# Which halves of K and V a decode kernel keeps, with new orders for all engines and wider moving operands at the end

## The chip, the core and the metric

The kernel runs on one core of a Trainium2 chip. The metric is device time in microseconds from one launch; the time before is the median of three runs. The profile is of one further execution.

## What is computed

Four tokens (one new position in each of four sequences) pass twice through the same attention block A and the same gated FFN block B, with a layer norm ahead of each. Attention reads a window of the last 2048 cached positions, for 8 KV heads of width 256, two query heads to each.

```python
def _A_ref(x, k_cache, v_cache, wq, wo):
    W = min(4096, max(256, Sk // 4))                 # 2048 of 8192
    q = (x @ wq).reshape(B, Sq, Hq, Dh).transpose(0, 2, 1, 3)
    k = jnp.repeat(k_cache[:, :, Sk - W:, :], rep, axis=1)
    v = jnp.repeat(v_cache[:, :, Sk - W:, :], rep, axis=1)
    p = softmax(einsum("bhqd,bhkd->bhqk", q, k) * Dh ** -0.5)
    return einsum("bhqk,bhkd->bhqd", p, v).transpose(0, 2, 1, 3).reshape(B, Sq, Hq * Dh) @ wo
def _B_ref(x, w_gate, w_up, w_down):
    return (silu(x @ w_gate) * (x @ w_up)) @ w_down
x = x + _A_ref(_layernorm(x), ...); x = x + _B_ref(_layernorm(x), ...)
x = x + _A_ref(_layernorm(x), ...); x = x + _B_ref(_layernorm(x), ...)
```

Both layers use the same K and V, since there is one cache. A window of K of one token and head is 1 MB in bf16, one of V too: 64 MB for 32 pairs (token, head), and 128 MB if everything is read once in each layer.

## The kernel before

**Pairs and groups.** The unit of work is a triple of digits: token, layer, head ("013" is token 0, layer 1, head 3). `PLAN` lists the 64 triples in 44 stages; "+" or "&" joins two triples of a stage into one group that is computed together, and "&" issues their score matmuls as two operations. There are 50 groups.

**Buffers.** `half` (variable `kv`) is a pool of 27 halves of 512 KB in SBUF. A K pair or a V pair takes two. `SLOTS` says which half each load goes to, in the order of loads. A load into a half waits until the last PE operation that reads the previous content is done: `scores` frees K, `pv` frees V. `WHOLE` lists the triples whose K comes in one load of 1 MB.

**Held halves.** What layer 0 has loaded may stay for layer 1. `KEEP_K` and `KEEP_V` say for each token how many of the heads that come last in layer 0 keep K and V: 5, 5, 4, 7 and 6, 5, 4, 3. That is 21 K pairs and 18 V pairs, 42 and 36 halves. The rest of layer 1 is loaded again. A held K is also transposed already.

**A group** (`group`, from line 817). DVE transposes K halves in place (`tr`, L841), POOL spreads the query (`qe`, L880), PE computes scores into a bank S (L874), DVE takes maxima (L890, L904), ACT the exponential (L908), PE turns it (L921), ACT copies it (L930), PE sums (L938) and multiplies with V (L952) into a bank Y, ACT and DVE gather the head (L968, L970), PE flips it (L976), DVE scales it into `oT` (L1006), and PE multiplies with wo into bank A (`out_proj`, L1018 as columns, L1026 as rows). Banks S come in twos, Y in threes, and A, Z and Z2 are single, eight in all.

**Between layers.** When a token's eight heads are done: `rows`, `residual`, `norm`, then the FFN (`ffn`, L720 and L748, for tokens 0 and 3 together with a waiting one; `ffn_row` for tokens 1 and 2), `norm` and `qproj` (L594 to L630), and only then that token's layer-1 groups.

**The end.** The last group is `316&310`. It has no `pv`; `vs` (L989) multiplies V as the stationary operand with 2 moving columns. Then the projections of its two heads go to bank A: `mean_proj` (L1051) computes the mean of the result ahead of the result itself, `out_proj` (L1018) the result, both with 1 moving column. `finale` does the last norm, the FFN of the waiting tokens (L1117, L1128, 32 moving columns by repeating), the transposed residual (L1172), the down projection (L1182) and the output.

**Order.** Everything is recorded as operations with dependences, and five tables of numbers, `SEQ_PE`, `SEQ_DVE`, `SEQ_ACT`, `SEQ_POOL`, `SEQ_SP`, set the order in which each engine issues them. All loads stand in `SEQ_SP`; of those that SP meets before it first has to wait, every second one from the third on is given to ACT, which issues them before anything else. An engine takes its operations strictly in order.

**Zero matmuls.** An entry "w7" in `SEQ_PE` is a matmul of 512 columns whose stationary operand is a column of zeros (`filler`, L1274). It adds zero to bank A; the number says after which of the other engines' accesses to that bank it stands, and the next such access waits for it. There are 339 of them among 895 operations of PE.

## Time and profile before

| | us |
|---|---|
| median of 3 runs | 287.97 |
| the runs | 287.32, 287.97, 290.81 |
| the profiled execution | 292.21 |
| its span, first to last instruction | 290.4 |
| PE busy in it | 251.9 |
| DVE, POOL, ACT busy | 192.0, 82.8, 62.9 |

The DMA queues moved 106.2 MB. Busy PE time is made of pipelined records that overlap, and 102.1 us of it are zero matmuls, so it does not say that PE is full. The strip of slices, the table by stage and the chain of waits stand in the prediction, where they are used. In a row of the table by stage, the count in brackets after a busy time is the number of instructions; in a row of the chain, the first number is the start and the second the duration; "issue" is time in which the engine waited for nothing that the profile shows.

### The profile page before, as it was taken

The page shows a single profiled execution, that of the slowest core. Times are in us where ns is not written, and L with a number is a line of the kernel's source. Part 1 is how long each engine was busy: PE and PEld are TensorE (multiplying, and loading weights), DVE is VectorE, ACT ScalarE, POOL GpSimd, SP SyncE. Part 2 cuts the span into 40 slices and gives each one's busy share as a digit, 9 for nine tenths or more (in the row PEclk, how much of TensorE's full clock was granted, in tenths as well). Part 3 has the DMA queues.
Part 4 walks back from the last instruction along what each step waited for, and adds up shares of the span by engine and source line. Part 5 has one row for each costly group of instructions (what it writes and reads, how often), then busy time and mean ns, then how long its engine had stood idle before and what let it go on. Part 6 is the DMA issues. An engine that isn't in the chain of part 4 may idle for free.

```text
span 290.4 us, 11178 instructions
## 1 busy us (share of the span) xinstructions
PE 251.9 (87%) x4933; PEld 141.6 (49%) x4933; DVE 192.0 (66%) x594; ACT 62.9 (22%) x178; POOL 82.8 (29%) x233
## 2 busy tenths in 40 slices
PE   3989799899898999798989898988869988879976
PEld 1434344544474454354544544454536546745675
DVE  5527756547353895887867479959697679556532
ACT  0012011121202132213223122313323231223400
POOL 0071003031024224122423231605233162245231
PEclk9999889999999999999899999999999999999957
DMA  7999999999997999999999999999999999999800
GB/s 278 420 423 417 406 415 396 402 408 403 391 402 235 368 408 416 413 414 401 349 320 407 383 418 407 408 410 374 381 387 373 415 405 353 332 342 395 350 5 0
DMA packets 29192, 106.20 MB, mean 366 GB/s; under 512 B 2900, under 2 KB 7000, under 8 KB 26840
## 3 DMA queue, kind: packets, MB, share of 16 engines
q1 hardware_dynamic: 27424, 96.12, 85.3%
q10 hardware_dynamic: 1720, 9.37, 7.9%
q8 instruction: 38, 0.62, 0.9%
q14 instruction: 10, 0.08, 0.1%
HBM read 105.48 MB, written 0.00 MB: 363 GB/s over the span
## 4 chain that ended last, share of the span: by engine, by line
PE 42%; DMA 34%; DVE 16%; issue 2%; ACT 2%; SPq 2%; POOL 1%; DVEq 0%; ACTq 0%
DMA half<-in_A_k_cache_dram 29%; PE A L1274 13%; DVE half L841 10%; PE S L874 7%; PE Y L952 6%; DMA half<-in_A_v_cache_dram 5%; PE A L1026 2%; PE Z L720 2%; DVE oh L970 2%; PE Y L921 2%; PE Z L748 1%; ACT oh L968 1%; PE A L1018 1%; DVE tiny L890 1%; SPq L851 1%
## 5 line engine op out<-in xcount | busy, mean ns | idle before, releaser
L841 DVE STREAM_TRANSPOSE half<-half 128x1024 uint32<-128x1024 uint32 x86 | 105.4, 1233 | 12.2 <-DMA half<-in_A_k_cache_dram 12.1
L1274 PE MATMUL A<-identb,small 128*128 128x512 bf16 x339 | 102.1, 401 | 5.3 <-DVE A L434 4.8
L965 POOL TENSOR_TENSOR small<-small 128x2 f32<-128x2 f32 (+1 forms) x50 | 39.2, 789 | 57.3 <-DVE small L943 55.4
L952 PE MATMUL Y<-half,pT 128*4 128x256 bf16 (+1 forms) x992 | 43.3, 272 | 6.3 <-DMA half<-in_A_v_cache_dram 3.7
L874 PE MATMUL S<-half,qe 128*8 128x128 bf16 (+1 forms) x1600 | 41.6, 236 | 6.7 <-DVE half L841 2.3
L1274 PEld LDWEIGHTS A<-identb,small 128*128 128x128 bf16 x339 | 29.4, 104 | 33.1 <-issue 12.0
L874 PEld LDWEIGHTS S<-half,qe 128*8 128x8 bf16 x1600 | 28.9, 85 | 18.8 <-DVE half L841 4.5
L908 ACT ACTIVATE praw<-S,small 104x128 bf16<-104x128 f32 (+1 forms) x50 | 19.8, 397 | 82.2 <-DVE small L904 73.7
L880 POOL TENSOR_TENSOR qe<-qc,tiny 128x64 bf16<-128x64 bf16 x64 | 17.9, 293 | 51.1 <-PE S L874 37.5
L970 DVE SCALAR_TENSOR_TENSOR oh<-oh,small,Y 128x256 bf16<-128x256 bf16 x49 | 23.1, 472 | 13.4 <-ACT oh L968 12.9
L968 ACT ACTIVATE oh<-Y 128x256 bf16<-128x256 f32 x49 | 18.7, 382 | 49.0 <-PE Y L952 43.6
L952 PEld LDWEIGHTS Y<-half,pT 128*4 128x4 bf16 (+1 forms) x992 | 18.4, 83 | 17.8 <-DMA half<-in_A_v_cache_dram 5.4
L890 DVE TENSOR_REDUCE tiny<-S 104x1 bf16<-104x128 f32 (+1 forms) x50 | 15.9, 318 | 6.0 <-PE S L874 5.9
L930 ACT ACTIVATE pT<-Y 128x64 bf16<-128x64 f32 (+1 forms) x50 | 12.6, 252 | 33.0 <-PE Y L921 28.5
L1026 PE MATMUL A<-wo_sb,oT 128*4 128x448 bf16 x200 | 16.7, 352 | 1.8 <-DVE oT L1006 1.7
L556 POOL TENSOR_SCALAR st<-st 128x1 f32<-128x1 f32 x15 | 4.0, 265 | 48.0 <-DVE st L546 47.9
L904 DVE TENSOR_REDUCE small<-S 104x1 f32<-104x32 f32 x50 | 8.8, 179 | 11.8 <-PE S L898 11.4
L1212 POOL MEMSET oT<- 128x16 bf16 x40 | 4.1, 112 | 40.1 <-PE A L1026 30.5
L943 DVE TENSOR_REDUCE small<-Y 128x2 f32<-128x32 f32 (+1 forms) x50 | 9.3, 188 | 8.8 <-PE Y L938 8.5
L1006 DVE TENSOR_TENSOR oT<-Y,small 128x4 bf16<-128x4 f32 (+1 forms) x63 | 8.9, 154 | 6.8 <-PE Y L976 5.3
L976 PEld LDWEIGHTS Y<-tiny,oh 128*128 128x128 bf16 x98 | 6.7, 100 | 10.9 <-DVE oh L970 6.0
L976 PE MATMUL Y<-tiny,oh 128*128 128x2 bf16 (+1 forms) x98 | 9.7, 168 | 2.5 <-DVE oh L970 2.1
(181 smaller groups left out, 272.5 us busy)
## 6 DMA issues: line engine op xcount, KB each, us to landing
half<-in_A_v_cache_dram SPq DMA_DIRECT2D x90, 512.0 KB, 7.8
half<-in_A_k_cache_dram SPq DMA_DIRECT2D x55, 512.0 KB, 7.3
half<-in_A_k_cache_dram SPq DMA_DIRECT2D x10, 1024.0 KB, 13.5
half<-in_A_k_cache_dram ACTq DMA_DIRECT2D x5, 1024.0 KB, 23.4
wo_sb<-in_A_wo_dram SPq DMA_DIRECT2D x7, 448.0 KB, 16.0
wq_sb<-in_A_wq_dram ACTq DMA_DIRECT2D x2, 1024.0 KB, 8.8
wd_sb<-in_B_w_down_dram SPq DMA_DIRECT2D x1, 1568.0 KB, 15.6
wg_sb<-in_B_w_gate_dram SPq DMA_DIRECT2D x1, 1344.0 KB, 9.1
```

Of the source, the lines that this page charges most:

```text
L841: return e.transpose(a, a)
L874: last = e.matmul(Sb[s_][qd:qd + 8, 0:32 * 2 * J], lhsT=qe[q_][:, P, ce, :, :].rearrange("p a n -> p (a n)"), rhs=keys(kcs[P], J * x, J, c ...
L880: g.op(POOL, "qe", lambda e, P=P, t=t, kvh=kvh: e.tensor_tensor(qe[q_][:, P, :, :, :], qc[t][:, kvh, :, :].unsqueeze(2).broadcast_to([128, ...
L890: g.op(DVE, f"max{n}", lambda e: e.tensor_reduce(pmax[s_][0:R, :], Sb[s_][0:R, 0:N], AX.X, ALU.max), r=(f"s{s_}",), w=(f"pmax{s_}",), bank ...
L908: return e.activation(praw[0:R, 0:128 * n].rearrange("p (g r l) -> p g r l", g=2 * n, l=2), Sb[s_][0:R, 0:128 * n].rearrange("p (l g r) -> ...
L952: last = e.matmul(Yb[p_][32 * gg:32 * gg + M, 256:512], lhsT=pT[pt][:, gg, 2 * a + hv, 4 * P:4 * P + M] if n == 2 else p1[:, gg % 2, 2 * a ...
L965: g.op(POOL, f"pow{n}", lambda e: e.tensor_tensor(ri[p_][:, 0:2 * n], rs[p_][:, 0:2 * n], expo[:, 1:1 + 2 * n], op=ALU.pow), r=(f"rs{p_}", ...
L968: g.op(SCA, "oh", lambda e: e.activation(oh[:, :], Yb[p_][:, 256:512], ACT.Copy), r=(f"y{p_}",), w=("oh",), bank=(f"Y{p_}",))
L970: g.op(DVE, "oho", lambda e: e.scalar_tensor_tensor(out=oh[:, :], in0=oh[:, :], scalar=lomask[:, 0:1], in1=Yb[p_][:, 256:512], op0=ALU.mul ...
L976: last = e.matmul(Yb[p_][:, 2 * n * dh:2 * n * dh + 2 * n], lhsT=oh[:, :].rearrange("p (m e) -> p e m", e=2)[:, dh, :], rhs=osel[:, 0:2 * ...
L1026: last = e.matmul(Ab[32 * k:32 * k + B, 0:D], lhsT=oT[oi][:, k % 2, k // 2, :], rhs=wo_sb[:, 4 * kvh + k, :], start=False, stop=False, ski ...
L1274: return e.matmul(Ab[:, 0:512], lhsT=zero[:, 0:1].broadcast_to([128, 128]), rhs=identb[:, :].unsqueeze(1).broadcast_to([128, 4, 128]), sta ...
```

## The change

`HELD` takes the place of the two `KEEP` tables. It names held K pairs and held V halves one by one:

```diff
-KEEP_K = (5, 5, 4, 7)
-KEEP_V = (6, 5, 4, 3)
+HELD = (
+    "0k1 0k3 0k4 0k5 0k6 0k7 0v11 0v30 0v31 0v40 0v41 0v50 0v51 0v60 0v61 0v70 0v71 1k3 1k4 1k5 1k6 1k7 1v01 1v30 "
...
+FILL = dict(w="A", z="Z", y="Z2", s="S0", t="S1")
```

That is 22 K pairs (6, 5, 4, 7 for tokens 0 to 3) and 37 V halves (11, 11, 8, 7), 81 halves. `group` asks for each V half by itself whether it is held:

```diff
-                    vs = [[], []]
-                    for hv, cell in enumerate(vs):
-                        g.tag = ("v", t, layer, kvh)
+                vs = [v_held.pop((t, kvh, hv)) if (t, kvh, hv) in v_held else [] for hv in range(2)]
+                new = [layer == 0 or f"{t}v{kvh}{hv}" not in held for hv in range(2)]
+                for hv, cell in enumerate(vs):
+                    if new[hv]:
+                        g.tag = ("v", t, layer, kvh, hv)
...
-                    if free_v[P]:
+                    if free_v[P][hv]:
                         o.rel = (vss[P][hv],)
```

`PLAN` has 46 stages with the same 50 groups: "002" and "005", and "015&014" and "105", are stages of their own, and three groups change between "+" and "&" (the last is now "316+310"). `WHOLE`, `SLOTS` and all `SEQ` tables are new. `SEQ_ACTQ` names the loads that ACT issues.

```diff
 PLAN = (
-    "000", "002 005", "004", "007", "006", "001", "003", "102", "100", "101", "013", "016", "011+104",
...
+    "000", "002", "005", "004", "007", "006", "001", "003", "102", "100", "101", "013", "016", "011+104", "015&014",
...
+SEQ_ACTQ = (
+    "49 214 260 48 47 112 145 146 194"
+)
...
-        for o in [o for o in fresh if not o.deps][2::2]:
+        odd = [self.ops[int(x)] for x in SEQ_ACTQ.split()]
+        for o in odd:
             order[SP].remove(o)
             o.eng = SCA
-            odd.append(o)
```

The start of the two queues that load. First what ACT issues, before and after:

```order
L506 DMA wq_sb<-in_A_wq_dram 128x4096 x2
L829 DMA half<-in_A_k_cache_dram 128x4096 x4
L835 DMA half<-in_A_k_cache_dram 128x2048
L851 DMA half<-in_A_v_cache_dram 128x2048
L506 DMA wo_sb<-in_A_wo_dram 128x2x896
L829 DMA half<-in_A_k_cache_dram 128x4096
L851 DMA half<-in_A_v_cache_dram 128x2048
```

```order
L520 DMA wq_sb<-in_A_wq_dram 128x4096
L843 DMA half<-in_A_k_cache_dram 128x4096
L520 DMA wo_sb<-in_A_wo_dram 128x2x896
L520 DMA wq_sb<-in_A_wq_dram 128x4096 x2
L520 DMA wg_sb<-in_B_w_gate_dram 128x896
L864 DMA half<-in_A_v_cache_dram 128x2048 x3
```

And what SP issues first, before and after (a wq load of 128x4096 is one of three pieces of 1 MB, that of 128x2048 the fourth, wq3, of 512 KB):

```order
L506 DMA wq_sb<-in_A_wq_dram 128x2048
L506 DMA wo_sb<-in_A_x_dram 4x448
L829 DMA half<-in_A_k_cache_dram 128x4096
L506 DMA wq_sb<-in_A_wq_dram 128x4096
L851 DMA half<-in_A_v_cache_dram 128x2048 x2
```

```order
L520 DMA wo_sb<-in_A_x_dram 4x448
L843 DMA half<-in_A_k_cache_dram 128x4096 x5
L520 DMA wq_sb<-in_A_wq_dram 128x2048
L520 DMA wo_sb<-in_A_wo_dram 128x2x896
L849 DMA half<-in_A_k_cache_dram 128x2048
```

The pieces of wq led both queues before; all but one now stand behind K pairs.

Zero matmuls may now go to five banks: w is A, z is Z, y is Z2, s and t are the two S banks. `epochs` lists the other engines' runs of accesses to a bank; an entry "z4" stands behind the fourth run and ahead of the fifth.

```diff
+    def epochs(self, b):
+        runs, pe = [], True
+        for o in self.ops:
+            if b in o.bank:
+                if o.eng != PE:
+                    if pe:
+                        runs.append([])
+                    runs[-1].append(o)
+                pe = o.eng == PE
+        return runs
...
-                if x[0] == "w":
-                    o, k = Op(len(self.ops), PE, "fw", filler), max(int(x[1:]), 1)
+                if x[0] in near:
+                    o, k, lst = Op(len(self.ops), PE, "fw", lambda e, b=FILL[x[0]]: filler(e, b)), int(x[1:]), near[x[0]]
```

There are 293 of them instead of 339: 82 in A, 73 in Z, 99 in Z2, 39 in S. Up to the first scores there are 51 (57 before), from there to the first gate matmuls of token 0's FFN 66 (126 before), and after that 176 (156 before). PE just before the first gate matmuls of that FFN (`ffn`, L720, now L734), before:

```order
L771 MATMUL Z<-tiny,wide 128x1 x8
L1274 MATMUL A<-identb,small 128x512
L895 MATMUL S<-small,identb 104x32
L898 MATMUL S<-identb,tiny 104x32
L1018 MATMUL A<-oT,wo_sb 128x1 x16
L1274 MATMUL A<-identb,small 128x512 x2
L938 MATMUL Y<-pT,tiny 128x32
L1274 MATMUL A<-identb,small 128x512 x3
L921 MATMUL Y<-sel,praw 64x32 x4
L1274 MATMUL A<-identb,small 128x512 x2
L540 MATMUL Z<-st,small 128x2
L1274 MATMUL A<-identb,small 128x512
```

and after:

```order
L785 MATMUL Z<-tiny,wide 128x1 x8
L990 MATMUL Y<-tiny,oh 128x2 x2
L1036 MATMUL A<-oT,wo_sb 128x1 x16
L1311 MATMUL A<-identb,small 128x512 x2
L966 MATMUL Y<-half,pT 4x256 x8
L554 MATMUL Z<-st,small 128x2
L1311 MATMUL S<-identb,small 128x512
L562 MATMUL Z<-xn,twice 128x1
L1311 MATMUL A<-identb,small 128x512 x4
```

Between the turn of token 0's rows and its gate matmuls stood nine zero matmuls and parts of another group; now there are seven, and little else.

At the end the moving operands of the last group's V (2 columns), of the two projections and of their mean (1 column) are repeated to 32 columns, and the projections go to an S bank instead of A (`last_proj`):

```diff
-                            x = e.matmul(Yb[p_][:, 2 * n * dh + 2 * P:2 * n * dh + 2 * P + 2],
+                            c0 = 32 * (n * dh + P)
+                            x = e.matmul(Yb[p_][:, c0:c0 + 32].rearrange("p (r n) -> p r n", n=2),
...
+            def rhs(k):
+                return oT[oi][:, k % 2, k // 2, t:t + 1].broadcast_to([128, 32])
...
+            def col(e):
+                x = None
+                for cc in range(4):
+                    c0 = 128 * cc if cc < 3 else D - 128
+                    for k in range(4):
+                        x = e.matmul(sb_[:, 32 * cc:32 * cc + 32], lhsT=wo_sb[:, 4 * kvh + k, c0:c0 + 128], rhs=rhs(k),
+                                     start=False, stop=False, skip_group_check=True)
+                return x
```

`finale` reads that S bank where it read A, and the residual is added once ahead of it (`xp`). PE at the end, from the last V matmuls, before:

```order
L989 MATMUL Y<-pT,half 128x2 x48
L771 MATMUL Z<-tiny,wide 128x1 x8
L989 MATMUL Y<-pT,half 128x2 x16
L540 MATMUL Z<-st,small 128x2
L1244 MATMUL A<-st,small 128x1
L1051 MATMUL A<-oT,wmb 128x1 x16
L1018 MATMUL A<-oT,wo_sb 128x1 x32
L548 MATMUL Z<-xn,twice 128x1
L1117 MATMUL Z<-xn,wg_sb 128x32 x28
```

and after:

```order
L554 MATMUL Z<-st,small 128x2
L1311 MATMUL S<-identb,small 128x512
L1004 MATMUL Y<-pT,half 128x32 x32
L785 MATMUL Z<-tiny,wide 128x1 x8
L1004 MATMUL Y<-pT,half 128x32 x32
L1311 MATMUL S<-identb,small 128x512
L1278 MATMUL S<-st,small 128x1
L1081 MATMUL S<-oT,wo_sb 128x32 x32
L1072 MATMUL S<-oT,wmb 128x32 x16
L1311 MATMUL S<-identb,small 128x512 x2
L1150 MATMUL Z<-xn,wg_sb 128x32 x28
```

The other token's statistic (L540, now L554) has moved ahead of the V matmuls, the mean behind the projections, and zero matmuls in an S bank stand between. Behind this, the transposed residual (L1172) moves ahead of the up matmuls, and one zero matmul stands behind the down projection.

108 lines of the change are left out of this document (56 added, 52 removed), and 173 rows, old and new, of tables (HELD, PLAN, SEQ_ACT, SEQ_DVE).

## The prediction

> **What bounds the kernel now.** I read the profile's strip of 40 slices first, because it shows which resource is full for how long.
>
> ```profile
> PEclk9999889999999999999899999999999999999957
> DMA  7999999999997999999999999999999999999800
> GB/s 278 420 423 417 406 415 396 402 408 403 391 402 235 368 408 416 413 414 401 349 320 407 383 418 407 408 410 374 381 387 373 415 405 353 332 342 395 350 5 0
> ```
>
> The 16 DMA engines are full from the first slice to the 38th; the last two slices (about 14.5 us) move nothing, and in them the TensorE clock is at 0.5 to 0.7. So the time has three parts: bytes at the full rate, four dents in the rate (slices 13, 20 and 21, 28 to 31, 34 to 38), and a tail without transfers. The table by stage puts sizes on them. Its columns are busy time of PE, weight loads, DVE, ACT and POOL, then granted clock, DMA share and GB/s.
>
> ```profile
> 60.00:80.00 20.00, 19.24 (x294) 9.06 (x293) 10.21 (x31) 3.57 (x12) 4.07 (x8) 1.00 1.03 400
> 80.00:100.00 20.00, 18.66 (x416) 11.43 (x415) 11.87 (x39) 3.42 (x11) 6.44 (x19) 1.00 0.90 328
> 140.00:160.00 20.00, 17.39 (x315) 9.00 (x313) 15.26 (x42) 6.24 (x15) 7.71 (x24) 0.98 0.95 358
> 200.00:220.00 20.00, 15.78 (x389) 8.83 (x377) 16.43 (x47) 6.35 (x16) 6.08 (x19) 1.00 0.99 377
> 240.00:260.00 20.00, 17.06 (x486) 11.99 (x487) 12.91 (x47) 4.69 (x14) 6.54 (x21) 1.00 0.96 339
> 275.00:280.00 5.00, 3.64 (x93) 3.11 (x91) 2.27 (x17) 0.54 (x1) 1.01 (x1) 0.72 0.08 24
> 280.00:285.00 5.00, 4.70 (x157) 4.62 (x155) 1.36 (x11) 0.55 (x2) 2.88 (x9) 0.50 0.01 3
> ```
>
> Against 400 GB/s the four dents cost 20 x (1 - 328/400) = 3.6, 2.1, 1.2 and 3.0 us, about 10 in all. They lie where a token passes from layer 0 to layer 1: its FFN and query projection hold up the groups that free buffer halves, and SP waits for those. PE looks busy there (18.66 of 20 us), but part of it is zero matmuls; the table of line 1274 alone (PE, weight loads, clock, DMA) shows how many:
>
> ```profile
> 0.00:29.00 29.00, 17.76 (x57) 5.68 (x57) 1.00 0.95 384
> 29.00:81.00 52.00, 33.95 (x126) 10.46 (x126) 0.97 1.03 403
> ```
>
> Then the chain of waits, for the tail (start, us, what):
>
> ```profile
> 275.86 0.76 PE Y L989 x27
> 276.62 1.18 issue
> 277.81 0.72 PE Y L989 x21
> 278.74 0.43 PE Y L989 x16
> 279.17 0.43 PE Z L540 x2
> 279.59 0.43 PE A L1244 x2
> 281.63 0.93 PE Z L1117 x28
> 282.95 0.44 PE A L1092 x2
> 283.40 0.46 PE Z L1128 x14
> 285.89 2.17 PE Y L1182 x28
> ```
>
> After the last V half has landed (near 275.4, by the DMA share of 0.08 from 275 to 280), PE is the path to the end, but for 1.18 us of "issue", in which it waited for nothing that the profile shows.
>
> **Bytes.** Held halves go from 78 (42 of K, 36 of V) to 81 (44 and 37), so three loads of this group fall away:
>
> ```profile
> half<-in_A_v_cache_dram SPq DMA_DIRECT2D x90, 512.0 KB, 7.8
> ```
>
> Three times 512 KB are 1.57 MB; at 400 GB/s -3.9 us. Bounds: 0, if buffers and not the rate set the pace; -4.6 at the 339 GB/s of 240 to 260. I take -3.9, since the DMA share is 0.9 or more in all but the tail.
>
> **Slots.** The pool stays at 27 halves. When a token ends layer 0 it holds 22, 20, 16 and 20 of them (tokens 0 to 3) before, and 23, 21, 16 and 21 after. Tokens 0, 1 and 3 thus have one half less to stream through just where the dents are: token 0 four instead of five. One half is 0.52 MB, 1.3 us of queue. Bounds: 0, and 1.3 us at each of the three, 3.9. I take half, +2.0, because each dent is many releases long and one half less in flight delays the first ones fully and the later ones hardly.
>
> **Token 0 earlier.** Between the first scores and the first FFN PE runs 126 zero matmuls before (the row above, 33.95 us by their pipelined records) and 66 after. These rows show what waited for what:
>
> ```profile
> 28.08 1.15 PE L874 MATMUL S<-half,qe 128*8 128x128 bf16 x64 [0.48 <-POOL qe L880]
> 80.93 1.48 PE L720 MATMUL Z<-xn,wg_sb 128*128 128x32 bf16 x42
> 86.01 1.90 PE L748 MATMUL Z<-wide,wd_sb 128*128 128x32 bf16 x56
> 67.35 0.43 SPq L506 DMA_DIRECT2D wd_sb<-in_B_w_down_dram  x1
> wd_sb<-in_B_w_down_dram SPq DMA_DIRECT2D x1, 1568.0 KB, 15.6
> ```
>
> The down weights landed at 67.35 + 15.6 = 82.95, and their matmuls began at 86.01: PE was 3.1 us late. After, 0.5 MB more stands ahead of these weights in the queues (1.3 us), so at most 1.8 us can come back: -1.8. Bounds -1.8 and 0. The zero matmuls removed cost nothing elsewhere; what hides them is DMA. If the first groups turn out to be paced by DVE and ACT, removing them brings 0, and if the clock falls without them there is a loss (last rival).
>
> **Start.** ACT now issues wq2, a K pair and a piece of wo before the rest of wq, SP five K pairs before wq3. The two queues before:
>
> ```profile
> wq_sb<-in_A_wq_dram ACTq DMA_DIRECT2D x2, 1024.0 KB, 8.8
> 22.13 0.39 PE L594 MATMUL Z<-wq_sb,st 128*4 128x512 bf16 x4
> ```
>
> 2 MB on one queue in some 10 us is half the full rate: the queues share evenly. After, wq3 ends 5.8 MB deep in SP's queue with as much beside it: 11.5 MB, 29 us. The last query matmuls stood at 22.13, so the first scores move from 28.08 to about 35. Cost 0: all 27 halves (14.2 MB) and 5.7 MB of weights, 20 MB or 50 us, are queued before SP meets its first wait for a free half, so the cover is 14 us. If it were gone, each further us would be paid.
>
> **Fewer transposes, more banks.** One more held K pair spares two transposes:
>
> ```profile
> L841 DVE STREAM_TRANSPOSE half<-half 128x1024 uint32<-128x1024 uint32 x86 | 105.4, 1233 | 12.2 <-DMA half<-in_A_k_cache_dram 12.1
> PE 42%; DMA 34%; DVE 16%; issue 2%; ACT 2%; SPq 2%; POOL 1%; DVEq 0%; ACTq 0%
> ```
>
> That is 2.5 us of DVE, of which DVE's 16% share of the chain would put 0.4 on the path: -0.4 (bounds 0, -2.5). Zero matmuls in S, Y and Z banks add waits: each must come between two uses of its bank by DVE or ACT, and all real matmuls queue behind it on PE. Line 1274 already obeys this on bank A, and idles 0.5 us beyond its first wait:
>
> ```profile
> L1274 PE MATMUL A<-identb,small 128*128 128x512 bf16 x339 | 102.1, 401 | 5.3 <-DVE A L434 4.8 <-DVE wide L763 0.4
> L1026 PE MATMUL A<-wo_sb,oT 128*4 128x448 bf16 x200 | 16.7, 352 | 1.8 <-DVE oT L1006 1.7
> ```
>
> I take 0; bound +1.9, if each of the 211 outside bank A idled as L1026 does (1.8 us in 200). The new plan, splits and slot numbers keep 50 groups; I take 0 with +-1.5, the size of the smallest dent.
>
> **Tail.** Prices at full clock come from these rows of the chain:
>
> ```profile
> 235.51 0.38 PE A L1026 x8
> 250.54 1.52 PE Z L748 x56
> 281.35 0.23 DVE xn L1073
> 139.51 0.22 PE Z L540 x2
> ```
>
> A full-width weight with 32 moving columns costs 1.52/56 = 27 ns. The 64 matmuls of line 989 took 1.91 us; at 27 ns 1.73: -0.2. The 1.18 us gap sits inside one of their runs and I cannot name it: -0.6, half (bounds 0, -1.2). The statistic of another token (line 540) moves ahead of them, into PE's wait for V: -0.43. The mean (line 1244) at 0.22: -0.2. One zero matmul before it and two after the projections, at some 0.22 each, of which DVE's 0.23 us for xn hides part of the pair: +0.4. Lines 1117 and 1128: 28 x 27 = 0.76 instead of 0.93, 14 x 27 = 0.38 instead of 0.46: -0.25. The variance (line 1092): -0.2. Line 1182: L1026 moved 8 x 448 columns in four strips in 0.38 us, 896 a strip; L1182 moves 28 x 224 in two, 3136 a strip, so 1.33 instead of 2.17: -0.85. The sum is -2.3; with the whole gap -2.9. At half clock the three zero matmuls cost twice as much (+1.1 beside xn) and only the moved statistic and half the gap are won: 0, and +0.6 without the gap, the upper end.
>
> All but the moves rests on the clock. The rows above have it at 0.50 while PE is busy 4.70 of 5 us with operands of 1, 2 and 32 columns, whereas L748 with 32 columns ran at 1.00 between full groups. I conclude that columns moved, not instructions, keep it up. A rule of the Trainium skill speaks against the widening: TensorE: Matmul & The Clock Gate, "Why this matters for your kernels", has throughput drop only where matmul bursts lie more than some 3 us apart. No such gap is in this tail, so by it the widening brings nothing; the row at 0.50 already disagrees. By that rule the tail term would be 0.
>
> **Sum.** -3.9 + 2.0 - 1.8 - 0.4 - 2.3 = -6.4 us. The profiled execution took 292.21 us (span 290.4 and 1.8 around it), so 285.8 by itself. It stood 4.24 above the median of the three runs, 287.97, which gives 281.6.
>
> **Rivals.**
> - Slots take all: 3.9 instead of 2.0, and token 0's lateness stays since PE isn't what delays it: 281.6 + 1.9 + 1.8 = 285.3. For it: the dents lie exactly there. Against: token 2, whose held count stays, has the smallest dent.
> - The clock stays at half in the tail (tail 0): 283.9. Against: L748's 1.00.
> - Token 0's dent of 3.6 closes altogether (1.8 beyond my term) and the whole gap goes (0.6): 279.2; with slots at no cost 277.2.
> - Slower than before, by the late start: if the 50 us between first scores and first FFN are set by DVE, ACT and the chains of the groups, not by zero matmuls, the 7 us pass through to token 0's FFN and the dent grows by them, and the 1.8 are not gained: 281.6 + 7 + 1.8 = 290.4. With the clock falling where zero matmuls are gone, several us more. It decides from the point where first scores to FFN take more than 46 us, beyond which token 0 is later than now. Against: zero matmuls are 34 of these 52 us of PE records.
>
> **How the numbers follow.** My forecast 0.40 (its own range 279 to 284.5, three quarters of it faster by over 2%), token 0's dent closed 0.16, slots take all 0.22, clock at half 0.07, late start 0.15 (half of it slower by over 2%). Two per cent, about what a measurement of this kernel can tell from no change, is 5.8 us: below 282.2 or above 293.7. Faster 0.40 x 0.75 + 0.16 = 0.46; slower 0.08; within 0.46. The range 276.5 to 289 leaves out most of the slow half of the late start (0.1) and the ends of the fast case (0.07).
>
> **What would show it.** Three half loads and two transposes fewer; first scores near 35 and the first gate matmuls by 81, no later; the rate of 80 to 100 not under 328 GB/s; granted clock near 1.0 to the end and the down projection at 1.3 us; the span after the last landing near 12.5 us instead of 15. Wrong if the rate of the dents falls by more than the 3.9 us won, or if token 0's gate matmuls come after 83.

## The result: slower by 5 per cent

The changed kernel takes 307.0 us (median of four runs, 303.1 to 309.7), the kernel before beside it 289.4. The ratio is 1.0515, interval [1.0346, 1.0685]; here and below ratios leave out runs that lie over 1.5 per cent above a kernel's fastest, which medians hold, so that the loss is some 15 us by the ratio and 17.6 by the medians. The prediction was 281.6. The profiled execution took 305.49 us, its span 303.6. The strip of 40 slices of the changed kernel (granted clock, DMA share, rate):

```profile
PEclk9997599999997997799999999978999999999999
DMA  7999999989994899998999999996999999799910
GB/s 285 420 421 407 413 411 401 406 314 359 396 358 148 322 388 421 412 384 318 335 368 394 391 371 393 351 324 245 376 397 414 406 366 301 237 341 340 405 41 3
```

The tail is shorter and its clock is full, as forecast, but the rate has more and deeper dents, and they begin earlier, in slice 9. The same in the table by stage of the changed kernel (busy time of PE, weight loads, DVE, ACT, POOL; clock, DMA share, GB/s):

```profile
60.00:80.00 20.00, 17.36 (x366) 8.93 (x363) 11.69 (x37) 5.54 (x20) 5.78 (x11) 1.00 0.94 356
80.00:100.00 20.00, 17.73 (x380) 10.89 (x384) 6.66 (x32) 2.76 (x7) 5.60 (x17) 0.91 0.77 279
140.00:160.00 20.00, 17.65 (x321) 9.11 (x322) 13.35 (x46) 5.13 (x14) 6.98 (x20) 1.00 0.94 333
200.00:220.00 20.00, 17.99 (x319) 9.32 (x319) 12.46 (x42) 4.42 (x11) 5.90 (x16) 0.83 0.85 315
240.00:260.00 20.00, 18.83 (x411) 10.91 (x407) 14.29 (x43) 4.66 (x15) 8.24 (x24) 1.00 0.90 326
260.00:280.00 20.00, 18.35 (x430) 10.90 (x426) 11.49 (x40) 5.64 (x16) 5.16 (x17) 1.00 0.92 319
```

Against 400 GB/s these six rows lose 2.2, 6.1, 3.4, 4.3, 3.7 and 4.1 us; the 23.6 us in all face some 10 before. The row of 80 to 100 was the one to watch: forecast not under 328, it shows 279.

At the start, the changed kernel's DVE and PE show what waits (timelines of the two engines, with the idle time before a row and what ended it):

```profile
10.64 1.25 DVE L855 STREAM_TRANSPOSE half<-half 128x1024 uint32<-128x1024 uint32 x1 [7.43 <-DMA half<-in_A_k_cache_dram]
...
15.02 0.59 PE L554 MATMUL Z<-st,small 128*128 128x2 f32 x2 [8.27 <-DVE st L551]
26.65 0.19 PE L562 MATMUL Z<-xn,twice 128*128 128x1 bf16 x1 [3.40 <-DVE st L560]
32.14 1.45 PE L608 MATMUL Z<-wq_sb,xn 128*4 128x512 bf16 x12 [1.74 <-DVE st L565]
41.58 0.63 PE L888 MATMUL S<-half,qe 128*8 128x128 bf16 x32
```

The kernel before, in the same view of PE:

```profile
8.00 0.58 PE L540 MATMUL Z<-st,small 128*128 128x2 f32 x2 [0.71 <-DVE st L537]
17.80 0.82 PE L594 MATMUL Z<-wq_sb,xn 128*4 128x512 bf16 x12 [1.33 <-issue]
```

A transpose of K stands fourth in DVE's new order, and DVE sat 7.43 us until that K had landed; constants and norms queued behind it, and further transposes stand between the norms. PE waited 8.27 and 3.40 us for the norm, the query came at 32.14 instead of 17.80, and the first scores at 41.58 instead of 28.08. The prediction had looked at the load queues alone and said 35.

At token 0's passage, SP's and PE's timelines of the changed kernel:

```profile
73.26 17.68 SPq L864 DMA_DIRECT2D half<-in_A_v_cache_dram  x5
...
83.51 1.46 PE L734 MATMUL Z<-xn,wg_sb 128*128 128x32 bf16 x42
90.17 0.39 PE L966 MATMUL Y<-half,pT 128*4 128x256 bf16 x8
91.62 2.73 PE L608 MATMUL Z<-wq_sb,xn 128*4 128x512 bf16 x24
94.83 0.39 PE L966 MATMUL Y<-half,pT 128*4 128x256 bf16 x8
96.02 0.39 PE L966 MATMUL Y<-half,pT 128*4 128x256 bf16 x8
```

The gate matmuls start at 83.51 (80.93 before). SP's five V loads wait from 73.26 on for halves. A half comes free with a product with V (L966): one at 90.17, and the next only at 94.83, behind a query projection that takes 2.73 us, with the granted clock at 0.50 over it. The down weights are late as well: SP issued them at 72.67 instead of 67.35, so they landed near 87.1, and their matmuls start at 87.63. The kernel before has products with V and the query projection interleaved, at full clock (its PE timeline):

```profile
88.01 0.39 PE L952 MATMUL Y<-half,pT 128*4 128x256 bf16 x8
88.92 0.39 PE L952 MATMUL Y<-half,pT 128*4 128x256 bf16 x8
89.94 0.82 PE L594 MATMUL Z<-wq_sb,xn 128*4 128x512 bf16 x12
90.59 0.39 PE L952 MATMUL Y<-half,pT 128*4 128x256 bf16 x8
90.81 0.82 PE L594 MATMUL Z<-wq_sb,xn 128*4 128x512 bf16 x12
91.90 0.39 PE L952 MATMUL Y<-half,pT 128*4 128x256 bf16 x8
```

Last, the end, from the changed kernel's chain of waits (start, us, what):

```profile
292.12 0.85 PE Y L1004 x32
293.18 0.82 PE Y L1004 x32
296.07 0.75 PE Z L1150 x28
297.46 0.46 PE Z L1161 x14
299.85 1.46 PE Y L1215 x28
```

The last bytes land near 290.8, 12.8 us before the end (14.5 before, where they land near 275.9). From the first V product of the last group to the end it is 11.5 us instead of 14.5, but PE is 1.3 us late for it.

To compare kernels, the rate in windows of 2 us was summed, and the time read off at which so many MB had moved. A stretch of 5 MB takes 12.0 to 12.3 us where the queues are full. The table holds the us that each stretch took, in one execution of each kernel, whose time stands in the last row (labels are explained below). The kernel before and two with the same loads and PE order, b_wide and b_slot, differ among themselves by up to 0.6 us in a stretch of 5 MB and by up to 1.0 in a longer one.

| MB | before | changed | b_late | b_less | b_one2 | b_hold | b_28 | b_hold28 | a_28 | a_all |
|---|---|---|---|---|---|---|---|---|---|---|
| 20 to 25 | 12.3 | 12.5 | 12.4 | 12.3 | 12.3 | 16.7 | 12.3 | 12.3 | 12.5 | 12.5 |
| 25 to 30 | 12.5 | 14.8 | 17.3 | 12.5 | 12.5 | 12.3 | 12.5 | 13.8 | 15.1 | 12.3 |
| 30 to 35 | 14.5 | 14.2 | 15.5 | 12.6 | 13.0 | 13.4 | 13.0 | 13.6 | 14.0 | 13.5 |
| 35 to 40 | 14.2 | 18.4 | 14.2 | 12.6 | 15.3 | 16.2 | 12.6 | 15.2 | 17.2 | 16.0 |
| 40 to 45 | 12.0 | 12.0 | 12.1 | 12.1 | 12.0 | 12.0 | 12.1 | 12.0 | 12.0 | 12.0 |
| 45 to 50 | 12.1 | 12.4 | 12.1 | 12.2 | 13.5 | 13.1 | 12.1 | 12.2 | 12.5 | 12.3 |
| 50 to 55 | 12.9 | 15.1 | 12.2 | 12.4 | 14.0 | 15.4 | 12.2 | 12.4 | 13.7 | 14.9 |
| 55 to 60 | 14.3 | 13.6 | 14.3 | 12.9 | 15.3 | 14.1 | 12.6 | 14.0 | 13.1 | 14.1 |
| 60 to 65 | 12.6 | 12.5 | 12.5 | 12.4 | 13.8 | 14.5 | 12.7 | 13.2 | 14.5 | 12.3 |
| 65 to 80 | 37.4 | 44.0 | 37.1 | 36.9 | 38.1 | 37.6 | 36.8 | 36.7 | 38.8 | 39.6 |
| 80 to 90 | 25.7 | 24.7 | 24.9 | 24.8 | 24.9 | 25.2 | 25.1 | 24.8 | 25.6 | 25.7 |
| 90 to 100 | 27.9 | 32.3 | 27.6 | 28.5 | 28.2 | 30.3 | 29.4 | 32.0 | 30.5 | 30.7 |
| reached 104 MB at | 269.5 | 287.6 | 273.0 | 266.0 | 273.5 | 281.8 | 264.4 | 273.9 | 281.2 | 277.7 |
| time of the execution | 292.2 | 305.5 | 295.3 | 288.2 | 293.0 | 298.7 | 287.0 | 290.4 | 297.3 | 293.8 |

The changed kernel is 18.1 us behind at 104 MB: 2.3 lost at 25 to 30, 4.2 at 35 to 40, 2.2 at 50 to 55, 6.6 at 65 to 80 and 4.4 at 90 to 100, and some 2 won back. Of the 18.1, 3.2 come back because it has less left to move, and 1.7 in the tail, which leaves the 13.2 between the two spans. The largest loss, at 65 to 80, lies at the passage of token 2, whose held halves are as before. So the question is not where one thing broke, but what makes the passages dearer.

### The profile page after: what moved, and what is told of

It is laid out like the page before. It is cut to its first block, busy times and chain, and to the rows that moved or that the text cites. A ratio compares the mean times of both kernels' runs of the same rounds, so it can differ in the third digit from the quotient of the medians.

```text
span 303.6 us, 11082 instructions
## 1 busy us (share of the span) xinstructions
PE 251.9 (83%) x4891; PEld 137.5 (45%) x4891; DVE 190.6 (63%) x592; ACT 63.7 (21%) x178; POOL 83.1 (27%) x231
## 2 busy tenths in 40 slices
DMA packets 28472, 104.63 MB, mean 345 GB/s; under 512 B 2820, under 2 KB 6920, under 8 KB 25864
## 4 chain that ended last, share of the span: by engine, by line
PE 41%; DMA 30%; DVE 21%; ACT 3%; issue 2%; POOL 2%; SPq 1%; DVEq 0%; ACTq 0%
DMA half<-in_A_k_cache_dram 18%; DVE half L855 13%; DMA half<-in_A_v_cache_dram 11%; PE S L888 7%; PE Y L966 7%; PE Z L1311 4%; PE A L1311 3%; DVE oh L984 2%; PE S L1311 2%; PE Z L734 2%; PE A L1044 2%; PE Y L935 1%; DVE tiny L904 1%; PE Z L608 1%; PE Z L670 1%
## 5 line engine op out<-in xcount | busy, mean ns | idle before, releaser
L855 DVE STREAM_TRANSPOSE half<-half 128x1024 uint32<-128x1024 uint32 x84 | 102.9, 1232 | 20.3 <-DMA half<-in_A_k_cache_dram 20.0
L1311 PE MATMUL Z<-identb,small 128*128 128x512 bf16 x172 | 55.0, 384 | 0.3 <-DVE xr L789 0.3
L966 PE MATMUL Y<-half,pT 128*4 128x256 bf16 (+1 forms) x992 | 44.8, 280 | 10.1 <-DMA half<-in_A_v_cache_dram 4.7
L894 POOL TENSOR_TENSOR qe<-qc,tiny 128x64 bf16<-128x64 bf16 x64 | 18.1, 294 | 63.5 <-PE S L888 45.3
L984 DVE SCALAR_TENSOR_TENSOR oh<-oh,small,Y 128x256 bf16<-128x256 bf16 x49 | 23.2, 472 | 14.5 <-ACT oh L982 14.3
L966 PEld LDWEIGHTS Y<-half,pT 128*4 128x4 bf16 (+1 forms) x992 | 18.2, 85 | 28.1 <-issue 8.5
L1311 PE MATMUL A<-identb,small 128*128 128x512 bf16 x82 | 27.9, 442 | 3.5 <-DVE A L448 3.3
L1311 PEld LDWEIGHTS Z<-identb,small 128*128 128x128 bf16 x172 | 14.4, 99 | 14.0 <-issue 6.7
L944 ACT ACTIVATE pT<-Y 128x64 bf16<-128x64 f32 (+1 forms) x50 | 12.5, 252 | 33.7 <-PE Y L935 31.7
L1044 PE MATMUL A<-wo_sb,oT 128*4 128x448 bf16 x204 | 18.5, 356 | 0.7 <-DVE oT L1024 0.5
L1311 PEld LDWEIGHTS A<-identb,small 128*128 128x128 bf16 x82 | 8.3, 115 | 13.5 <-issue 7.2
L1311 PE MATMUL S<-identb,small 128*128 128x512 bf16 x39 | 13.6, 387 | 0.2
L554 PE MATMUL Z<-st,small 128*128 128x2 f32 x30 | 6.1, 274 | 9.2 <-DVE st L551 8.4
```

Of the source, the lines that this page charges most:

```text
L855: return e.transpose(a, a)
L894: g.op(POOL, "qe", lambda e, P=P, t=t, kvh=kvh: e.tensor_tensor(qe[q_][:, P, :, :, :], qc[t][:, kvh, :, :].unsqueeze(2).broadcast_to([128, ...
L944: g.op(SCA, f"pt{n}", lambda e: e.activation(pf, Yb[p_][:, 0:PW], ACT.Copy), r=(f"yp{p_}",), w=(f"pT{pt}",), bank=(f"Y{p_}",))
L966: last = e.matmul(Yb[p_][32 * gg:32 * gg + M, 256:512], lhsT=pT[pt][:, gg, 2 * a + hv, 4 * P:4 * P + M] if n == 2 else p1[:, gg % 2, 2 * a ...
L984: g.op(DVE, "oho", lambda e: e.scalar_tensor_tensor(out=oh[:, :], in0=oh[:, :], scalar=lomask[:, 0:1], in1=Yb[p_][:, 256:512], op0=ALU.mul ...
L1044: last = e.matmul(Ab[32 * k:32 * k + B, 0:D], lhsT=oT[oi][:, k % 2, k // 2, :], rhs=wo_sb[:, 4 * kvh + k, :], start=False, stop=False, ski ...
```

## Experiments

Names with a_ are the changed kernel with something set back, names with b_ the kernel before with something of the change. Medians over all runs, and the ratio to the kernel before in the same session with its 95% interval. Runs of one kernel scatter by 2 to 4 us each way. Differences between kernels are best read from the ratios, of which 0.01 is 2.9 us.

| kernel | median us (runs) | ratio |
|---|---|---|
| changed | 307.0 (4) | 1.052 [1.035, 1.069] |
| a_start | 305.5 (4) | 1.058 [1.050, 1.065] |
| a_dve | 309.0 (4) | none: its runs lie between 301 and 314 |
| a_start2 | 305.5 (5) | 1.045 [1.037, 1.053] |
| b_late | 295.1 (4) | 1.017 [1.007, 1.028] |
| a_fillA | 317.9 (4) | 1.090 [1.077, 1.104] |
| b_less | 291.7 (4) | 1.010 [1.001, 1.019] |
| a_clk | 303.8 (4) | 1.054 [1.033, 1.074] |
| b_wide | 289.2 (10) | 0.997 [0.990, 1.003] |
| b_hold | 300.0 (4) | 1.042 [1.035, 1.049] |
| b_hold2 | 301.1 (6) | 1.036 [1.022, 1.049] |
| b_hold13 | 301.4 (5) | 1.047 [1.040, 1.054] |
| b_one | 297.8 (4) | 1.035 [1.030, 1.041] |
| b_one2 | 295.4 (6) | 1.027 [1.018, 1.035] |
| b_slot | 288.9 (12) | 0.997 [0.992, 1.002] |
| b_28 | 285.1 (10) | 0.995 [0.990, 1.000] |
| b_hold28 | 289.7 (4) | 1.012 [0.997, 1.027] |
| a_28 | 300.0 (4) | 1.052 [1.034, 1.070] |
| a_all | 293.8 (4) | 1.020 [1.015, 1.026] |

The kernel before stood at 288.3 to 290.0 in these sessions.

### The late start

b_late changes only DVE's order in the kernel before: transposes among the norms.

```diff
-19 39 44 ... 35 9 52 53 ... 43 63 73 56 83 ... 42 64 ... 7 76 77 79 143 86 87 89 192 ...
+19 39 44 ... 35 9 143 52 53 ... 43 144 63 73 56 83 ... 42 118 119 64 ... 7 192 191 76 77 79 215 86 87 89 ...
```

> The kernel before with nothing but the late start: the first transposes of four K pairs stand between the norms in DVE's order, so that the norms wait for K to land as they do in the changed kernel; queues, slots and all else as before. First scores go from 28 to about 38 to 41 us. Late start as the cause: the first wait for a free half grows and token 0's FFN is late, 4 to 7 us more than the 288 to 289 before. If 20 MB of queued loads cover it, as the prediction had it, the time stays within 1.5 us.

Measured: the group of the first score matmuls in b_late (count, then ns, then first and last start) begins at 37.2, and the first gate matmuls at 86.9, 6 us late; 295.1 us, 1.7% over the kernel before (0.7 to 2.8).

```profile
L874 PE MATMUL S<-half,qe x192: 216/218/232, 37.2 to 59.0; 128*8 128x128 bf16 x192
```

Nine us of lateness cost about 5 (2 to 8). The cover of 14 us that the prediction saw in the queues did not hold: its stretch of 25 to 30 MB takes 17.3 us instead of 12.5, so the transfers already stood still there. SP's timeline of the kernel before says why: three loads of V take it 12.77 us from 52.20 on, most of it waits for halves, so the cover was nearly used up before anything was late.

```profile
52.20 12.77 SPq L851 DMA_DIRECT2D half<-in_A_v_cache_dram  x3
```

a_start puts the seven transposes behind the norms and wq in front of both queues.

```diff
 SEQ_DVE
-19 3 2 240 38 52 ... 9 143 56 ... 11 119 168 66 ... 89 105 ...
+19 3 2 38 52 ... 9 56 ... 11 66 ... 89 240 143 119 168 118 144 239 105 ...
 SEQ_SP
-46 238 49 166 214 142 ... 47 50 ...
+50 46 49 238 166 214 142 ...
 SEQ_ACTQ
-49 214 260 48 47 112 145 146 194
+47 48 214 260 112 145 146 194
```

> The changed kernel with its start set back: the first seven transposes of K stand behind the four norms in DVE's order instead of between the constants, and the pieces of wq lead both queues again (wq3, x and wq2 on SP, wq0 and wq1 on ACT). Everything after is as changed. Late start as the cause of the loss: first scores come back from 41.6 to about 28 to 30 us, SP's waits of 15 and 18 us at 55 and 73 us shrink, the dents of 60 to 120 us give back the 5 to 6 us by which they exceed those of the kernel before, so 301 us against 307. Slots and orders as the cause: the first scores come early, but the same waits for free halves follow, since the halves come free only with token 0's FFN: within 2 us of 307.

a_dve has the first of these edits alone.

> The changed kernel with only DVE's order set back at the start (the seven transposes behind the four norms); the queues stay as changed. If the norms behind K transposes are what made the start late, the query matmuls come as soon as wq has landed, and the first scores stand near 35 us, where the prediction had them; that is half of the way back, 303 to 305 us if the late start costs, 307 if it does not. If wq is what is late, the first scores stay at 41 us.

Measured: a_start 305.5 us, but it did not do what it was made for: the transposes now stood ahead of the query's copy, and DVE waited for K there (3.66 and 3.63 us); first scores at 39.6. In a_dve they came at 38.5, not at 35, and its four runs gave 301 to 314 us, which decides nothing. a_start2 leads with K of heads 2 and 0, takes transposes as K lands, and keeps bank Z free between query and first scores.

```diff
 SEQ_SP
-46 238 49 166 214 142 260 117 48 190 47 50 ...
+50 46 142 49 166 190 238 214 260 117 48 47 ...
 SEQ_ACTQ
-49 214 260 48 47 112 145 146 194
+47 48 117 214 260 112 145 146 194
 SEQ_PE, between the query and the first scores (SEQ_DVE and SLOTS change to match)
-106 z4 z4 z4 z4 z4 z4 z4 w1 z4 ...
+106 w1 w1 w1 w1 w1 w1 w1 w1 w1 ...
```

> The changed kernel with its start set back in full, which the first two runs did not reach (first scores at 39.6 and 38.5 us): K of heads 2 and 0 leads the queues beside wq, DVE does the four norms before all but one transpose and then takes transposes as they land, and the zero matmuls between the query and the first scores go to bank A again. All from there on is as changed. First scores near 30 to 32 us. By the table of time per 5 MB the changed kernel loses 2.3 us between 25 and 30 MB; if that is what the late start costs, this one takes about 304 to 305 us. If the late start is what loses the 17 us, it takes under 298. If it costs nothing, 307.

Measured: first scores at 34.5, gate at 81.31, 30 MB at 76.1 instead of 78.0 us; ratio 1.045 instead of 1.052. The traced run lost its lead again: 104 MB came at 287.4, against 287.6. So the late start costs the changed kernel some 2 us at most, which the intervals do not tell from nothing, and is not what loses 15. Seven us at the first scores were two at the gate; why so few, no run shows.

### Zero matmuls

a_fillA leaves out the 211 in banks Z, Z2 and S:

```diff
-"w1 51 ... z4 106 z4 z4 ... y11 150 ... t11 ... s25 ..."
+"w1 51 ... 106 ... 150 ..."
```

> The changed kernel without its 211 zero matmuls in banks Z, Z2 and S; the 82 in bank A stay, the result is the same. Zero matmuls in other banks as the cause: each makes real matmuls queue behind a hand-over of its bank, and takes 0.22 to 0.4 us of PE where the real work is late, so without them PE reaches the work that frees halves earlier, 5 to 10 us less than 307 at an unchanged clock. Clock theory: PE's granted clock falls under 0.9 in the stages of layer 1 and groups take longer: 2 to 6 us more than 307. No effect (what the prediction took): within 2 us.

Measured: 317.9 us. Its strip of granted clock:

```profile
PEclk9997765775589576556658655777679695999987
```

The mean clock falls from 0.955 to 0.745, and the loss, 11 us, is about twice the upper end of what the clock theory forecast. That the zero matmuls wait for hardly any hand-over of a bank can be read in the changed kernel's groups (busy and mean ns, then idle time before them):

```profile
L1311 PE MATMUL Z<-identb,small 128*128 128x512 bf16 x172 | 55.0, 384 | 0.3 <-DVE xr L789 0.3
L1311 PE MATMUL A<-identb,small 128*128 128x512 bf16 x82 | 27.9, 442 | 3.5 <-DVE A L448 3.3
L1311 PE MATMUL S<-identb,small 128*128 128x512 bf16 x39 | 13.6, 387 | 0.2
```

PE idled 0.3, 3.5 and 0.2 us before them, 3.3 of it once at the start. Whether real work behind them comes later these rows do not show, and a_fillA cannot, since its clock fell. b_less leaves 66 of the 126 between first scores and first FFN in the kernel before, spread evenly.

```diff
-126 entries w between the first scores and the first gate matmuls
+66
```

> The kernel before with 66 instead of 126 zero matmuls between the first scores and the first gate matmuls, every second one left out, as many as the changed kernel has there; the result is the same. The prediction's term: token 0's FFN 1.8 us earlier, 1.8 us less. Clock theory: the granted clock falls under 0.9 between 30 and 95 us, the groups take longer, the FFN comes no earlier, and the time is 1 to 5 us more. No effect: within 1 us, since DVE, ACT and DMA set this stretch.

Measured: gate at 77.6 instead of 80.9, and the dents of token 0 nearly close (30 to 40 MB in 25.2 us instead of 28.7). The down matmuls start 2.9 us earlier, at 83.11, after a wait of 0.26 us for their weights: PE had indeed been late there. But the clock fell elsewhere, in the traced run to 0.63 and 0.52 at 244 to 252 us (windows of 4 us), with mean clocks of 0.93 to 0.96 in its runs, and at the end nothing is won: 1.010 [1.001, 1.019]. a_clk goes the other way and adds 43 where PE stood idle.

```diff
-... 938 901 918 939 1076 961 ...
+... 938 901 918 w8 w8 w8 w8 939 1076 961 ...
 and 24 more such places, as many as 0.8 of the idle time holds at 0.225 us each
```

> The changed kernel with 43 zero matmuls more, all in bank A, each in a place where PE stood idle for 0.3 us or more in the changed kernel's trace between 58 and 280 us. Clock theory (the granted clock falls to 0.5 to 0.7 at 92, 116, 124 and 200 us because PE has too little to do just ahead, and the FFN and query of a passage then take twice as long): the four dips go or shrink, mean clock 0.97 or more, 302 to 304 us. If the dips are no cause of the loss, 306 to 308; if the added matmuls hold up real ones, 308 to 310.

Measured: 104 MB at 284.7 instead of 287.6, 303.8 us by the median; but the ratio, 1.054, is not lower than the changed kernel's, and two of the four dips stayed (0.75 at 112, 0.65 at 200, in windows of 4 us). A gain of about 3 us is possible and not shown.

### The wide end

```diff
-x = e.matmul(Yb[p_][:, 2 * n * dh + 2 * P:2 * n * dh + 2 * P + 2], ..., rhs=pT[...] (2 columns)
+x = e.matmul(Yb[p_][:, c0:c0 + 32] ..., rhs=pT[...].unsqueeze(1).broadcast_to([128, 16, 2]))
 and last_proj, finale and the order of the last group as changed
```

> The kernel before with only the end as changed: 32 moving columns in the last product with V, in the projections of the last group and in its mean, these in an S bank, two zero matmuls behind them, the other token's statistic ahead. The two traces have the span behind the last landing at 14.3 us before and 12.3 after. If the wide end is worth what they show, 2 us less than before, granted clock at 1.0 to the end. If the clock in the end hangs on the kernel's rest, the same time as before, with the clock at 0.5 to 0.7.

Measured: 0.997 [0.990, 1.003]. The table by stage of b_wide has the clock at 1.00 in the tail, where the kernel before had 0.72 and 0.50:

```profile
275.00:280.00 5.00, 4.75 (x137) 4.00 (x135) 2.60 (x19) 0.58 (x2) 2.36 (x6) 1.00 0.02 4
280.00:285.00 5.00, 5.00 (x157) 4.44 (x155) 1.92 (x14) 0.55 (x2) 1.69 (x5) 1.00 0.01 3
```

Its last bytes land near 275.2 and the span ends at 288.5, 13.3 us after instead of 14.5. About 1 us, half of what was forecast, in the trace; the times do not tell it from none. Nor does the wide end always keep the clock: in 6 of the 17 traced kernels that have it (a_fillA, b_one, b_hold2, b_hold13, b_28, b_hold28) the clock falls to between 0.50 and 0.57 for some us behind the last landing, as it does in all three with the narrow end (before, b_late, b_less).

### The held set and its halves

b_hold is b_wide with the 81 held halves, in the kernel before's orders; the five loads and two transposes that fall away leave the tables, two V halves that are no longer held come in, and slots are numbered anew.

```diff
-0k1 0k3 0k4 0k6 0k7 0v1 0v3 .. 0v7 | 1k3..7 1v0 (none) 1v3..7 | 3v1 3v3 3v4
+0k1 0k3 0k4 0k5 0k6 0k7 0v11 0v3 .. 0v7 | 1k3..7 1v01 1v3..7 | 3v10 3v3 3v4 3v7
```

> The kernel before with the end and the held halves as changed (the 81 of the changed kernel, three loads and two transposes fewer), in the orders of the kernel before; only the slot numbers are new. By the prediction's terms, bytes -3.9, slots +2.0, transposes -0.4, it takes 2.3 us less than the kernel before with the wide end, about 284.5. If the held set and its slots are what loses the 17 us, it stands near 300. In between (289 to 292) slots take back all that the bytes give.

Measured: 300.0 us and a ratio of 1.042, against 289.2 and 0.997 with the wide end alone. The held set with its slot numbers, without a new order, costs 13 us by the ratios (10.8 by the medians) although it moves 3.9 us fewer bytes. One part is not its own: SP waited 14.87 us at two K loads of 1 MB, whose slots come free late in this numbering (SP's timeline of b_hold):

```profile
48.88 14.87 SPq L843 DMA_DIRECT2D half<-in_A_k_cache_dram  x2
64.27 3.98 SPq L864 DMA_DIRECT2D half<-in_A_v_cache_dram  x3
```

b_hold2 renumbers the first slots so that this load waits for an earlier release, b_slot renumbers those of b_wide alone.

```diff
 SLOTS only
```

> The kernel before with the wide end and the 81 held halves again, with new slot numbers for the first loads. In the first try (300 us) a K load of 1 MB at 25 MB stood in two halves that came free only behind a score matmul 70 places later than others, and everything behind it in SP's queue waited: 4.2 us between 20 and 25 MB that belong to that slot table and not to the held set. Now that load waits for an earlier release. If the rest stays as it was, 13.3 - 4.2 = 9 us behind the kernel with the wide end at 104 MB and 3.9 us of bytes saved, 294 to 296 us. If the early wait was also what made the later dents, 286 to 290, and the prediction's slots term of 2 us holds.

> The kernel before with the wide end and nothing else but new slot numbers for its 27 halves, by which loads wait less: the bytes queued between a load and what must land before its half comes free, short of 3 MB, sum to 32 MB instead of 42. If it is the distance between a load and the release it waits for that sets the dents, 1 to 3 us less than with the wide end alone, 286 to 288; if not, the same.

Measured: b_hold2 has 20 to 25 MB in 12.3 us again, but loses it later: 301.1 us, ratio 1.036. b_slot: 0.997, the same as b_wide, so other slot numbers need not change anything; in b_hold and b_one they did. b_hold13 leaves token 0's halves as they were:

```diff
-0k1 0k3 0k4 0k5 0k6 0k7 0v11 0v30 ... (as in b_hold)
+0k1 0k3 0k4 0k6 0k7 0v10 0v11 0v30 ... (token 0 as before)
```

> The kernel before with the wide end, and of the new held set only the parts of tokens 1 and 3 (80 held halves, two loads fewer); token 0 holds what it held before. With all 81 it was 300 us, with the old 78 some 289. If the half more of token 0 is what costs, 287 to 290. If every token's passage pays for its own half, two thirds of the loss stay: 295 to 298.

Measured: 301.4 us. It missed both expectations: token 0's half costs nothing that shows here, those of tokens 1 and 3 cost all. Then a single V half of token 1 (79 held, one load less), first with the early wait in its slot numbers (b_one, 297.8), then without:

```diff
-1v3 1v4 1v5 1v6 1v7
+1v01 1v3 1v4 1v5 1v6 1v7
```

> The kernel before with the wide end and one V half more held, of token 1 (79 held, one load of 512 KB fewer). Bytes: -1.3 us. The half is missing from the pool from token 0's passage to token 1's layer 1. By the prediction's price (about 1 us for a half at one passage) it takes 0 to 1 us less than with the wide end alone, 288 to 289. By the price that 28 halves showed (4 us for a half over all passages of the kernel before) 1 to 2 us more, 290 to 291.

> The kernel before with the wide end and one V half more held, again with the first loads' slots mended (the first try lost 3.5 us between 20 and 25 MB by the same kind of wait, 297.8 us). If one half costs what 28 halves gave back (4 us over all passages) less 1.3 us of bytes, 291 to 293; by the prediction's price, 288 to 289; if it stays at 296 or more, a half of token 1 is dearer than one of the pool.

Measured: b_one2 295.4 us, 1.027 [1.018, 1.035], 3.0 points or some 8.5 us above b_wide; above what was expected, and below the 296 from which a half of token 1 would have been dearer than one of the pool. Its column in the table by stretches shows part of it: it is 1.1, 1.4, 1.1, 1.0 and 1.2 us longer than the kernel before at 35 to 40, 45 to 50, 50 to 55, 55 to 60 and 60 to 65 MB, 5.8 in all, and 1.5 shorter at 30 to 35. That is where the half is held, though at 40 to 45 nothing is lost: by the order of loads it comes near 34 MB, and the load that it saves stood near 64.

### One half more

In three kernels the last 512 KB of wq are not loaded and the first columns stand in for them, which makes room for a 28th half.

```diff
-NPOOL = 27
+NPOOL = 28
-wq_sb = sb("wq_sb", [128, 3 * 4096 + 2048], BF16)
+wq_sb = sb("wq_sb", [128, 3 * 4096], BF16)
```

> The changed kernel with 28 halves instead of 27 and slot numbers to match; the room comes from wq's last 512 KB, which are not loaded (the first columns of wq stand in for them), so 0.5 MB and 1.3 us less to move. Nothing else differs. Slots theory (the loss is that too few halves are free where tokens pass from layer 0 to layer 1): the dents at 35 to 40, 50 to 55 and 90 to 95 MB, 10 us together, mostly close, 295 to 299 us against 307. Orders theory (PE and DVE themselves do the freeing work too late): one half more moves the wait by 1.3 us at each passage but the lateness stays, 302 to 306 us.

> The kernel before with the wide end and the 81 held halves (300 us with 27 halves) with 28 halves, the last 512 KB of wq left out in the same way. If the held set costs time because it leaves one half less at tokens 0, 1 and 3, one half more brings the whole cost back: 285 to 288 us. If the orders of the kernel before just don't fit another held set, it stays above 296.

> The kernel before with the wide end and 28 halves, the last 512 KB of wq left out in the same way: what one half is worth in the kernel before. By the prediction's price of a half (2.0 us at the passages of three tokens, bounds 0 and 3.9) and 1.3 us of bytes, 3 us less than with the wide end alone, 284 to 285. If all dents of the kernel before (10 us) come from a lack of halves, 279 to 281.

Measured: b_hold28 1.012 [0.997, 1.027] against 1.042 and 1.036 with 27: the missing half is worth 7 to 9 us there, 1.3 us of bytes in it, and what its new slot numbers are worth (b_one and b_one2, which differ in nothing else, lie 0.9 per cent apart). It is not all: with 28 halves and 81 held, as many are free at a passage as with 27 and 78, and yet it stands 1.5% above b_wide with 5.2 us fewer bytes. b_28: 0.995 against 0.997, so the kernel before hardly gains from a half more; in the traced run it reaches 104 MB 5.1 us earlier. a_28: 300.0 by the median, 104 MB at 281.2 instead of 287.6; the ratio of 1.052 [1.034, 1.070] shows no gain, though all four runs, 297.3 to 302.7, lie below the changed kernel's lowest, 303.1. By the traces 6.4 of the 18.1 us come back, 5.2 of them at 65 to 80 MB; by the ratio that is not shown.

### Three repairs at once

a_all is the changed kernel with 28 halves, a_start2's start and a_clk's zero matmuls.

```diff
 a_28 + a_start2 + a_clk
```

> The changed kernel with three repairs at once: 28 halves (the last 512 KB of wq left out), the start of the second repaired start, and the 43 zero matmuls in PE's idle places. At 104 MB these stood 6.4 (28 halves) and 2.9 us (zero matmuls) ahead of the changed kernel, and the start was 1.9 us ahead at 30 MB. If they are three separate causes, they add: 307 - 1.3 - 6.4 - 2.9 - 1.9 = 294 to 295 us, and the rest to the kernel before with 28 halves (285) is the new plan and orders. If they are one cause (a wait for the same halves), the sum falls short: 298 to 300. If the start's lateness was what the other two paid for, more: under 291.

Measured: 293.8 us, 1.020 [1.015, 1.026], what three separate causes give. 104 MB come at 277.7, 9.9 us earlier than in the changed kernel; the three parts had 6.4, 2.9 and, for the start, 0.2 there. It is still 7 us slower than b_28 by the ratios (8.7 by the medians), with the same pool and 3.9 us more bytes to move there. No kernel here beats the one before: b_wide and b_slot are equal to it, and b_28 leaves out a part of wq.

## Why the prediction was wrong

**Bytes, -3.9: right as bytes.** 104.63 instead of 106.2 MB were moved, and full stretches run at 12.0 to 12.3 us for 5 MB in both kernels. The DMA share that the term rests on is not 0.9 or more everywhere ahead of the tail, though: the strip has it at 0.7 in slice 13.

**Slots, +2.0 (bounds 0 and 3.9): the step that failed.** In the old orders the held set costs 13 us net by the ratios, that is 13 + 3.9 = some 17 us against the bytes (10.8 and 15 by the medians). The prediction charged a half once, at the passage of the token that holds it, with 1.3 us at most, and even halved it "because each dent is many releases long". One half of token 1 alone costs some 8.5 us. In its trace five of the six stretches from its load to its use are 1.0 to 1.4 us longer, about one transfer of 1.3 us each, at other tokens' passages too; what it saves is one transfer. These 5.8 us stand against 8.5 + 1.3 = 9.8 that it costs without the bytes saved; where the rest goes, and that SP waits for halves in each of the five, is not shown. Nor is it shown why 28 halves bring back only part: that the loads' order no longer fits is a guess. The clock may have a part in it: at token 1's passage b_hold's is at 0.50 for 6 us (142 to 148) and b_wide's for 2 (138 to 140), and no run separates cause and effect there.

**"The new plan, splits and slot numbers", 0 +- 1.5: failed too.** Every traced kernel with the new plan and orders takes 38.8 to 44.3 us for 65 to 80 MB, every one with the old ones 36.7 to 38.5, whether it holds 78, 79, 80 or 81 halves. The changed kernel's largest loss, 6.6 us, is there, at the passage of token 2, for which the held count did not change and slots were charged nothing. Its FFN runs at half the clock there (PE's timelines; the first row is the changed kernel's, the second that of the kernel before):

```profile
203.66 1.02 PE L670 MATMUL Z<-wg_sb,xn 128*4 128x512 bf16 x9
196.76 0.60 PE L656 MATMUL Z<-wg_sb,xn 128*4 128x512 bf16 x9
```

In a_28, with the same orders, the clock stays at 1.00 there and the stretch takes 38.8. In turn, three of the five stretches that b_one2 pays for (45 to 50 and 55 to 65) are hardly longer or even shorter in the changed kernel than before. So the price of the held set in the old orders can't be carried over place by place.

**Token 0 earlier, -1.8: right in kind, too small, and used up.** b_less shows 3.3 us at the gate, 2.9 at the down matmuls, and a nearly closed dent. In the changed kernel the late start took it: gate at 83.5, down weights landed near 87.1. And where zero matmuls were gone the clock fell elsewhere.

**Start, 0 under a cover of 14 us: wrong, some 2 us at most here.** First scores at 41.6 instead of 35, because DVE waits for K ahead of the norms; the prediction followed the queues and not DVE's order. b_late shows that the cover does not hold. The rival "late start" had the right mechanism with the wrong point of decision: first scores to FFN took 42 us, under its 46, and token 0 was later than before all the same.

**Transposes, -0.4.** Two fewer (84 instead of 86 at 1232 ns); not separable.

**Zero matmuls in other banks, 0: right as to the hand-overs** (0.5 us idle before them outside bank A). Their number and place matter: 11 us without the 211, perhaps 3 us by a_clk, which is not shown.

**Tail, -2.3: right in kind, half in size.** The clock is at 1.00 to the end, the first V product to the end takes 3.0 us less, and the down projection 1.46 us instead of 2.17 (1.33 forecast). PE comes 1.3 to 1.7 us late to it after the last landing, so 1.2 to 1.7 us are won in the traces and 0.9 by b_wide's ratio (between a gain of 2.8 and a loss of 0.9). The conclusion on which it rested, that columns moved keep the clock up, is not borne out: the clock fell with the wide end too, in 6 of 17 traces, and in the rows of 202 to 206 us in the last section it stays at 0.50 while L670 moves 512 columns a matmul.

By the ratios the bytes, the held set, the start and the tail give -3.9 + 17 + 2 - 1 = 14 of 15 us. That the sum comes out is partly luck, since the places do not agree. Which part of the loss the held set has in the changed kernel's own orders stays open: no run has these orders with the old held set.

## What to carry to other kernels

A buffer that stays held can cost at every wait for buffers between its load and its use, and not once: here one half of 512 KB cost about its transfer time, 1.0 to 1.4 us, in five stretches, and saved one transfer. So read from the rate first how many such waits lie in between, and try the new held set alone, in the old orders. Follow a moved operation in the order of the engine that executes it, not only in the queue that feeds it: one operation that waits for a transfer holds back all behind it. Filler work has two sides, and both have to be measured: here 60 zero matmuls ahead of an FFN made it 3.3 us late, and yet without them the kernel as a whole was not faster, because the clock fell elsewhere.
